# A ScalarE copy of the third product in three blocks of the last token half: what it does to the tail of an attention and maxout kernel

## The chip, the cores and the metric

The kernel runs on one core of one Trainium2 chip. The metric is the time of one execution on the device in microseconds (us). The runs of the kernel before lie within 1.2 us, so every statement below about hundredths of a us is about a stage inside one profiled execution, not about a total.

## The reference

```python
def _attn_ref(q, k, v, tau):                      # B, N, C = 4, 6144, 256
    qn = q / (norm(q, axis=1) + 1e-6); kn = k / (norm(k, axis=1) + 1e-6)
    a = softmax(kn.transpose(0, 2, 1) @ qn / tau)  # 256 x 256 for each batch
    return v @ a

def _moe_ref(x, w1, w2, w3, w_out):               # 24576 tokens, 256 -> 768 -> 256
    h = np.maximum(np.maximum(x @ w1, x @ w2), x @ w3)
    return h @ w_out
```

The function names `norm` and `softmax` stand for the written-out lines of the original. The second part, the maximum of three products and one more product, is nearly all of the work, and the change touches its last piece.

## The kernel before

The kernel folds the attention matrix into the three weights, so that each token needs three products with 256 x 768 weights, a maximum of the three, and a product with `w_out`. Tokens come in chunks of 512. For each 128-wide slice of the 768 columns, `h_block` makes three products in PSUM, the memory that takes TensorE's results, and takes their maximum with ScalarE and VectorE. In this cut and the next, three dots mark what is left out:

```python
    ps_h = ctx.enter_context(tc.tile_pool(name="ps_h", bufs=6, space=bass.MemoryType.PSUM))
    ...
    def h_block(gi, aw, fc, tsl=slice(0, TPC)):
        ...
        hp = []
        for m in range(3):
            t = htile(f"h_ps{m}")[:, :n]
            for ic in range(CC):
                PE.matmul(t..., lhsT=aw[m][:, ic, fsl], rhs=vt[:, tsl, ic, :],
                          start=(ic == 0), stop=(ic == CC - 1))
            hp.append(t)
        s_mx = mx_pool.tile([P, CHUNK], BF16, name="s_mx")[:, :n]
        ACT.activation(out=s_mx, in_=hp[0], func=AF.Copy)                  # L383
        DVE.tensor_tensor(out=s_mx, in0=hp[1], in1=s_mx, op=ALU.max)       # L384, first max
        DVE.tensor_tensor(out=ht, in0=hp[2], in1=s_mx, op=ALU.max)         # L385, second max
```

The products live in a pool of six PSUM banks. A product may be written only once the bank that it was given has been read by its last reader. The last chunk of 512 tokens is done in two halves of 256, so that the output of the first half can leave while the second is computed:

```python
        for fc in range(FC):                       # FC = 6 blocks of the first half
            h_block(gi, aw, fc, slice(0, HT))
            if 1 <= fc <= len(pending):
                pending[fc - 1]()                  # output products of the chunk before
        for fc in range(FC):                       # 6 blocks of the last half
            h_block(gi, aw, fc, slice(HT, TPC))
            if fc >= FC - HT:
                first_half(fc - (FC - HT))         # output products of the first half
        pss = [htile("o_ps") for _ in range(HT)]
        for fcs in (range(FC - 1), (FC - 1,)):
            for i in range(HT):
                products(pss[i], HT, i, fcs)       # output products of the last half
        ...                                        # two copies and two transfers out
```

"Block" below is one call of `h_block` in the last chunk; blocks 0 to 5 are the six of the last half.

Of the kernel before, what the change touches and what calls it, by code (L numbers as in the profile page):

```python
# [11 lines left out]
BF16 = mybir.dt.bfloat16  # L12
FP8 = mybir.dt.float8e4
AF = mybir.ActivationFunctionType
ALU = mybir.AluOpType
# [16 lines left out]
def kernel(  # L32
# [14 lines left out]
    DVE = nc.vector  # L47
    ACT = nc.scalar
# [6 lines left out]
    P = 128  # L55
    CC = C // P
    FC = d_ff // P
    CHUNK = 512
    TPC = CHUNK // P
# [20 lines left out]
    mx_pool = ctx.enter_context(tc.tile_pool(name="mx", bufs=4))  # L80
# [4 lines left out]
    def htile(name):  # L85
        return ps_h.tile([P, 512], FP32, tag="h", name=name)

    def xtile(name, cols=512, dtype=FP32):
        return ps_x.tile([P, cols], dtype, tag="x", name=name)
# [191 lines left out]
    def alloc_aw():  # L281
        return [aw_pool.tile([P, CC, d_ff], BF16, name=f"aw{m}_sb", tag=f"aw{m}") for m in range(3)]
# [83 lines left out]
        DVE.tensor_copy(out=vt[:, half:, :], in_=ps[:, half:, :])  # L366
        ACT.activation(out=vt[:, :half, :], in_=ps[:, :half, :], func=AF.Copy)

    def h_block(gi, aw, fc, tsl=slice(0, TPC)):

        vt = vts[gi]
        n = (tsl.stop - tsl.start) * P
        ht = hts[gi][:, fc, tsl.start * P:tsl.stop * P]
        fsl = slice(fc * P, (fc + 1) * P)
# [4 lines that stand above are left out]
                PE.matmul(t.rearrange("p (t n) -> p t n", n=P), lhsT=aw[m][:, ic, fsl], rhs=vt[:, tsl, ic, :],  # L379
                          start=(ic == 0), stop=(ic == CC - 1))  # L380
            hp.append(t)
        s_mx = mx_pool.tile([P, CHUNK], BF16, name="s_mx")[:, :n]
        ACT.activation(out=s_mx, in_=hp[0], func=AF.Copy)  # L383
        DVE.tensor_tensor(out=s_mx, in0=hp[1], in1=s_mx, op=ALU.max)  # L384
        DVE.tensor_tensor(out=ht, in0=hp[2], in1=s_mx, op=ALU.max)  # L385

    def o_steps(gi):

# [25 lines left out]
    def last_chunk(gi, aw, pending):  # L414

        hts[gi] = ht_pool.tile([P, FC, CHUNK], BF16, name="ht_sb")
        o_sb = o_pool.tile([P, TPC, d_model], FP32, name="o_sb")
        dst = out_r[gi // NCH, gi % NCH]
        HT = TPC // 2

        def products(ps, t0, i, fcs):
            c0 = i * d_model if t0 == 0 else 0
            for fc in fcs:
                PE.matmul(ps[:, c0:c0 + d_model], lhsT=hts[gi][:, fc, (t0 + i) * P:(t0 + i + 1) * P],  # L424
                          rhs=wo_sb[:, fc, :], start=(fc == 0 and c0 == 0), stop=(fc == FC - 1),
                          skip_group_check=True)

        first = {}

        def first_half(i):  # L430
            if i == 0:
                first["ps"] = xtile("o_ps")
            products(first["ps"], 0, i, range(FC))
            if i == HT - 1:
                ACT.activation(out=o_sb[:, 0:HT, :].rearrange("p t d -> p (t d)"), in_=first["ps"], func=AF.Copy)
                SP.dma_start(out=dst[:, 0:HT, :], in_=o_sb[:, 0:HT, :])

        for fc in range(FC):
            h_block(gi, aw, fc, slice(0, HT))
            if 1 <= fc <= len(pending):  # L440
                pending[fc - 1]()
        for fc in range(FC):
            h_block(gi, aw, fc, slice(HT, TPC))
            if fc >= FC - HT:
                first_half(fc - (FC - HT))
        pss = [htile("o_ps") for _ in range(HT)]
        for fcs in (range(FC - 1), (FC - 1,)):
            for i in range(HT):
                products(pss[i], HT, i, fcs)
        ACT.activation(out=o_sb[:, HT, :], in_=pss[0][:, 0:d_model], func=AF.Copy)  # L450
        DVE.tensor_copy(out=o_sb[:, HT + 1, :], in_=pss[1][:, 0:d_model])  # L451
        ACT.dma_start(out=dst[:, HT, :], in_=o_sb[:, HT, :])
        SP.dma_start(out=dst[:, HT + 1, :], in_=o_sb[:, HT + 1, :])
# [8 lines left out]
    aw = alloc_aw()  # L462
# [15 lines left out]
    for b in range(B):  # L478
# [3 lines left out]
        for ch in range(NCH):  # L482
            gi = b * NCH + ch
            if gi == B * NCH - 1:
                last_chunk(gi, aw, pending)
                break
# [23 lines left out]
            if more and 0 <= s0 < 8:  # L510
                g0 = s0 * 6
                for i, (which, g) in enumerate(((1, g0), (1, g0 + SQW), (0, g0), (0, g0 + SQW))):

                    last = not early and s0 == 7 and which == 0
# [17 lines left out]
            for fc in range(FC):  # L532
                h_block(gi, aw, fc)
                for f in gaps[fc]:
                    f()
# [12 lines left out]
            if more and ch == NCH - 1:  # L548
                et, rinv = st["e"], st["r"]
                aw = alloc_aw()  # L550
# [37 lines left out]
```

## Time and profile before

| | before |
|---|---|
| median of the first 3 runs | 573.58 us (573.29 to 574.51) |
| span of the profiled execution | 571.6 us |
| TensorE busy | 553.2 us, 97% |
| 36 products, 560.11 to 564.58 | 4.47 us (3.94 us if nothing waits) |
| from the first output product (564.58) to the end of TensorE's work (568.02) | 3.44 us |

A profile is read here in three steps. First, which engine is busy nearly all the time: TensorE. Second, where that engine is not: the chain of work that ended last names other engines only at the very start (GpSimd and the transfers of q) and in the last ten microseconds. Third, what ends those waits. The prediction below shows the lines. One more way of seeing a wait is worth learning. Matmuls are pipelined, and two undisturbed ones in a row cover 0.38 us in the timeline. Asked for in windows so narrow that only two show, the three waits of the kernel before are these lines (start, duration, count at the end):

```profile
561.85 0.38 PE L379 MATMUL h_ps<-vt_sb,aw_sb 128*128 128x256 bf16 x2
561.96 0.52 PE L379 MATMUL h_ps<-vt_sb,aw_sb 128*128 128x256 bf16 x2
562.76 0.59 PE L379 MATMUL h_ps<-vt_sb,aw_sb 128*128 128x256 bf16 x2
563.62 0.58 PE L379 MATMUL h_ps<-vt_sb,aw_sb 128*128 128x256 bf16 x2
```

The first line is an undisturbed pair. The others are longer by 0.14, 0.21 and 0.20 us, ahead of blocks 2, 3 and 4. That sums to 0.55 us, against 0.53 us by the count of matmuls in the prediction; the difference is rounding of the printed times.

What each wait is for can be read from the program after it is built: a product names the instruction whose end frees its bank. For block 2's first product, for example, that is the second max of the first half's last block, and for block 3's the second max of block 0. VectorE's second maxes of that stretch:

```profile
561.74 0.42 DVE L385 TENSOR_TENSOR ht_sb<-h_ps,s_mx 128x256 bf16<-128x256 f32 x1
562.60 0.42 DVE L385 TENSOR_TENSOR ht_sb<-h_ps,s_mx 128x256 bf16<-128x256 f32 x1
563.46 0.42 DVE L385 TENSOR_TENSOR ht_sb<-h_ps,s_mx 128x256 bf16<-128x256 f32 x1
```

TensorE goes on at 562.22 and 563.08, which is 0.06 us after the first of these maxes ends and 0.06 after the second.

ScalarE had idle time. In its timeline the value in brackets is its idle time before the instruction:

```profile
562.63 0.38 ACT L383 ACTIVATE s_mx<-h_ps 128x256 bf16<-128x256 f32 x1 [0.41 <-PE h_ps L379]
563.49 0.38 ACT L383 ACTIVATE s_mx<-h_ps 128x256 bf16<-128x256 f32 x1 [0.48 <-PE h_ps L379]
564.34 0.38 ACT L383 ACTIVATE s_mx<-h_ps 128x256 bf16<-128x256 f32 x1 [0.47 <-PE h_ps L379]
```

### The profile page before, as it was taken

The page shows a single profiled execution, that of the slowest core. Times are in us where ns is not written, and L with a number is a line of the kernel's source. Part 1 is how long each engine was busy: PE and PEld are TensorE (multiplying, and loading weights), DVE is VectorE, ACT ScalarE, POOL GpSimd, SP SyncE. Part 2 cuts the span into 40 slices and gives each one's busy share as a digit, 9 for nine tenths or more (in the row PEclk, how much of TensorE's full clock was granted, in tenths as well). Part 3 has the DMA queues.
Part 4 walks back from the last instruction along what each step waited for, and adds up shares of the span by engine and source line. Part 5 has one row for each costly group of instructions (what it writes and reads, how often), then busy time and mean ns, then how long its engine had stood idle before and what let it go on. Part 6 is the DMA issues. An engine that isn't in the chain of part 4 may idle for free.

```text
span 571.6 us, 9437 instructions
## 1 busy us (share of the span) xinstructions
PE 553.2 (97%) x3343; PEld 329.7 (58%) x3344; DVE 416.1 (73%) x658; ACT 309.5 (54%) x540; POOL 233.4 (41%) x237
## 2 busy tenths in 40 slices
PE   3789999999999999999999999999999999999997
PEld 2665555555755555555575555555575555555566
DVE  0048777877887778777767777777768778778775
ACT  1044567677464576776535467767645444444443
POOL 2441357776450078776560058776750000000000
PEclk9999999999999999999999999999999999999999
DMA  9995999884579168884279339984437233132112
GB/s 144 106 172 95 136 239 133 159 134 110 107 86 182 56 116 154 134 150 104 57 131 151 100 81 138 148 141 101 119 86 155 75 78 107 56 104 63 56 55 76
DMA packets 76960, 65.64 MB, mean 115 GB/s; under 512 B 52464, under 2 KB 62576, under 8 KB 76784
## 3 DMA queue, kind: packets, MB, share of 16 engines
q0 software_dynamic: 19072, 26.48, 38.6%
q1 hardware_dynamic: 57696, 38.41, 24.6%
q8 instruction: 26, 0.43, 0.3%
q14 instruction: 22, 0.18, 0.1%
q10 hardware_dynamic: 144, 0.13, 0.1%
HBM read 78.64 MB, written 25.17 MB: 182 GB/s over the span
## 4 chain that ended last, share of the span: by engine, by line
PE 93%; DMA 5%; POOL 0%; issue 0%; DVE 0%; POOLq 0%
PE h_ps L379 65%; PE o_ps L399 22%; DMA q_sb<-in_q_dram 5%; PE gram L250 3%; PE ew_ps L301 3%; POOL k_sb L99 0%; PE o_ps L424 0%; PE ew_ps L325 0%; PE warm_ps L459 0%; PE vt_ps L362 0%; PE gram L181 0%; DVE ht_sb L385 0%; DVE o_sb L451 0%; PE rs_ps L289 0%; PE gram L183 0%
## 5 line engine op out<-in xcount | busy, mean ns | idle before, releaser
L379 PE MATMUL h_ps<-vt_sb,aw_sb 128*128 128x512 bf16 (+1 forms) x1764 | 406.7, 375 | 0.1
L379 PEld LDWEIGHTS <-aw_sb 128*128 128x128 bf16 x1764 | 171.7, 98 | 161.7 <-DVE aw_sb L307 2.4
L384 DVE TENSOR_TENSOR s_mx<-h_ps,s_mx 128x512 bf16<-128x512 f32 (+1 forms) x294 | 198.9, 676 | 82.0 <-ACT s_mx L383 81.8
L383 ACT ACTIVATE s_mx<-h_ps 128x512 bf16<-128x512 f32 (+1 forms) x294 | 172.4, 586 | 124.1 <-PE h_ps L379 123.1
L385 DVE TENSOR_TENSOR ht_sb<-h_ps,s_mx 128x512 bf16<-128x512 f32 (+1 forms) x294 | 200.3, 681 | 30.6
L209 POOL TENSOR_TENSOR acc<-acc,sq 128x768 f32<-128x768 f32 x88 | 144.2, 1648 | 69.3 <-ACT sq L201 53.3
L399 PE MATMUL o_ps<-wo_sb,ht_sb 128*128 128x256 bf16 x1128 | 153.9, 273 | 0.0
L399 PEld LDWEIGHTS <-ht_sb 128*128 128x128 bf16 x1128 | 110.4, 98 | 52.1
L402 ACT ACTIVATE o_sb<-o_ps 128x512 f32<-128x512 f32 x94 | 56.1, 597 | 83.7 <-PE o_ps L399 83.7
L110 POOL DMA_DIRECT2D v_sb<-in_v_dram x48 | 27.8, 584 | 37.6 <-DMA vt_sb<-v_sb 35.4
L201 ACT ACTIVATE sq<-q_sb 128x768 bf16<-128x768 fp8e4 x48 | 40.5, 844 | 0.0
L201 ACT ACTIVATE sq<-k_sb 128x768 bf16<-128x768 fp8e4 x48 | 40.1, 835 | 0.0
L206 POOL CAST acc<-sq 128x768 f32<-128x768 bf16 x6 | 4.9, 820 | 65.0 <-ACT sq L201 65.0
L102 POOL DMA_DIRECT2D q_sb<-in_q_dram x33 | 18.4, 566 | 4.7 <-DMA v_sb<-in_v_dram 3.9
L169 PE MATMUL kk<-k_sb 128*128 128x256 fp8e4 x48 | 7.5, 338 | 11.8 <-DVE k_sb L155 6.4
L99 POOL DMA_DIRECT2D k_sb<-in_k_dram x29 | 16.1, 557 | 2.8 <-issue 1.1
L250 PE MATMUL gram<-k_sb,q_sb 128*128 128x512 fp8e4 x144 | 16.8, 276 | 0.0
L304 ACT ACTIVATE aw_sb<-ew_ps,rinv 128x384 bf16<-128x384 f32 (+1 forms) x24 | 13.2, 555 | 5.7 <-PE ew_ps L301 4.8
L250 PEld LDWEIGHTS <-q_sb 128*128 128x256 fp8e4 x144 | 15.9, 136 | 0.6
L222 POOL PARTITION_ALL_REDUCE tot<-acc x6 | 10.9, 1858 | 11.8 <-issue 5.9
L301 PE MATMUL ew_ps<-w_sb,et 128*128 128x384 bf16 (+1 forms) x96 | 15.6, 313 | 0.0
L181 PE MATMUL gram<-k_sb,q_sb 128*128 128x512 fp8e4 x48 | 11.4, 331 | 2.8 <-DMA q_sb<-in_q_dram 2.7
(64 smaller groups left out, 113.3 us busy)
## 6 DMA issues: line engine op xcount, KB each, us to landing
out_dram<-o_sb SPq DMA_DIRECT2D x41, 512.0 KB, 2.9
v_sb<-in_v_dram POOLq DMA_DIRECT2D x48, 256.0 KB, 4.1
k_sb<-in_k_dram POOLq DMA_DIRECT2D x24, 192.0 KB, 5.7
q_sb<-in_q_dram POOLq DMA_DIRECT2D x24, 192.0 KB, 7.1
out_dram<-o_sb SPq DMA_DIRECT2D x13, 256.0 KB, 2.0
k_sb<-in_k_dram POOLq DMA_DIRECT2D x5, 256.0 KB, 10.7
w_sb<-in_moe_w_dram POOLq DMA_DIRECT2D x9, 128.0 KB, 5.7
kf<-in_k_dram SPq DMA_DIRECT2D x1, 1024.0 KB, 4.9
```

The lines of the kernel that those rows point to most:

```text
L102: POOL.dma_start(out=qk[b][0][:, g0:g0 + w, :], in_=q_r[b][:, g0:g0 + w, :])
L110: POOL.dma_start(out=t, in_=v_r[gi // NCH, gi % NCH])
L201: ACT.activation(out=sq, in_=src, func=AF.Square)
L209: POOL.tensor_tensor(out=acc, in0=acc, in1=sq, op=ALU.add)
L250: PE.matmul(g[:, j * C:(j + 1) * C], lhsT=qt[:, tsl, j * P:(j + 1) * P], rhs=kt[:, tsl, :], start=(tp == 0 and j == 0), stop=(tp == NG // ...
L301: PE.matmul(ew[:, :w], lhsT=et[:, j, ic * P:(ic + 1) * P], rhs=w_sb[m][:, j, fsl], start=(j == 0), stop=(j == CC - 1))
L379: PE.matmul(t.rearrange("p (t n) -> p t n", n=P), lhsT=aw[m][:, ic, fsl], rhs=vt[:, tsl, ic, :], start=(ic == 0), stop=(ic == CC - 1))
L383: ACT.activation(out=s_mx, in_=hp[0], func=AF.Copy)
L384: DVE.tensor_tensor(out=s_mx, in0=hp[1], in1=s_mx, op=ALU.max)
L385: DVE.tensor_tensor(out=ht, in0=hp[2], in1=s_mx, op=ALU.max)
L399: PE.matmul(st["ps"][:, half], lhsT=ht[:, fc, t * P:(t + 1) * P], rhs=wo_sb[:, fc, :], start=(fc == 0), stop=(fc == FC - 1))
L402: ACT.activation(out=st["o"][:, t - 1:t + 1, :].rearrange("p t d -> p (t d)"), in_=st["ps"], func=AF.Copy)
```

## The change

The intent is to give VectorE less to do where TensorE waits for it. A second ScalarE copy puts the third product into SBUF as bf16, so the second max has both inputs there.

```diff
-    def h_block(gi, aw, fc, tsl=slice(0, TPC)):
+    def h_block(gi, aw, fc, tsl=slice(0, TPC), two_copies=False):
...
         DVE.tensor_tensor(out=s_mx, in0=hp[1], in1=s_mx, op=ALU.max)
-        DVE.tensor_tensor(out=ht, in0=hp[2], in1=s_mx, op=ALU.max)
+        last = hp[2]
+        if two_copies:
+            last = mx_pool.tile([P, CHUNK], BF16, name="s_h2")[:, :n]
+            ACT.activation(out=last, in_=hp[2], func=AF.Copy)
+        DVE.tensor_tensor(out=ht, in0=last, in1=s_mx, op=ALU.max)
...
         for fc in range(FC):
-            h_block(gi, aw, fc, slice(HT, TPC))
+            h_block(gi, aw, fc, slice(HT, TPC), two_copies=fc in (0, 2, 3))
```

The copy does two things at once. It makes the second max cheaper, and it frees the third product's PSUM bank without VectorE. Both kernels were built and their instructions compared engine by engine: apart from block 0's new copy, with the bank that it frees and the max that reads it, they are the same up to block 1 of the last half; from block 2 on the banks are handed out differently, and TensorE waits for other instructions.

## The prediction

> **What bounds the kernel now.** I read the page first, then the last microseconds: the change touches six blocks of the last chunk only (here a block is the three products of one 128-wide slice of d_ff for 256 tokens). From the page:
>
> ```profile
> PE 553.2 (97%) x3343; PEld 329.7 (58%) x3344; DVE 416.1 (73%) x658; ACT 309.5 (54%) x540; POOL 233.4 (41%) x237
> PEclk9999999999999999999999999999999999999999
> PE 93%; DMA 5%; POOL 0%; issue 0%; DVE 0%; POOLq 0%
> ```
>
> TensorE is busy 97% of the span at full clock, and 93% of the chain that ended last is TensorE; VectorE shows as 0%. So nearly all of the 573.58 us cannot be reached by a VectorE change. The question is what happens where this rule fails: in the tail. The chain that ended last, in order of time, for the last 17 us (start, duration, what):
>
> ```profile
> 559.61 0.66 PE o_ps L399 x6
> 560.27 2.34 PE h_ps L379 x20
> 562.61 0.43 DVE ht_sb L385
> 563.03 0.04 issue
> 563.08 0.82 PE h_ps L379 x6
> 563.89 0.03 issue
> 563.92 0.81 PE h_ps L379 x6
> 564.74 0.66 PE o_ps L424 x6
> 565.39 0.66 PE h_ps L379 x6
> 566.05 1.98 PE o_ps L424 x18
> 568.03 0.02 issue
> 568.05 0.42 DVE o_sb L451
> ```
>
> Here TensorE once waits for a second max (L385 at 562.61), and after that the blocks take 0.82 us in place of 0.66. The weight loads of the same stretch show all waits (in brackets: idle before):
>
> ```profile
> 562.22 0.64 PEld L379 LDWEIGHTS <-aw_sb 128*128 128x128 bf16 x6 [0.16 <-issue]
> 563.08 0.64 PEld L379 LDWEIGHTS <-aw_sb 128*128 128x128 bf16 x6 [0.22 <-issue]
> 563.93 0.53 PEld L379 LDWEIGHTS <-aw_sb 128*128 128x128 bf16 x5 [0.21 <-issue]
> ```
>
> Three waits, 0.59 us together. Counted by matmuls it is a little less: in the timeline 36 of them start from 560.11 and the next kind starts at 564.58; at the undisturbed pitch of 0.109 us (six in 0.656, as 564.58, 565.23 and 565.89 show) they would need 3.94, so 4.47 - 3.94 = 0.53 us is lost. I use 0.53. After 564.58 nothing is lost: the last 18 start at 565.89 and end at 568.02. So **0.53 us is the most that the change can win**, 0.09% of the time.
>
> The cause is VectorE's pace. Groups by form:
>
> ```profile
> L385 DVE TENSOR_TENSOR ht_sb<-h_ps,s_mx 128x512 bf16<-128x512 f32 x282 | 195.2, 692 | 29.4
> L385 DVE TENSOR_TENSOR ht_sb<-h_ps,s_mx 128x256 bf16<-128x256 f32 x12 | 5.1, 425 | 1.2
> L384 DVE TENSOR_TENSOR s_mx<-h_ps,s_mx 128x256 bf16<-128x256 f32 x12 | 5.0, 417 | 1.0 <-ACT s_mx L383 1.0
> L383 ACT ACTIVATE s_mx<-h_ps 128x256 bf16<-128x256 f32 x12 | 4.6, 383 | 4.8 <-PE h_ps L379 3.9 <-DVE ht_sb L385 0.9
> ```
>
> In the timeline VectorE's starts in the last half go 562.08 (first max), 562.60 (second), 562.94, 563.46 and so on: 0.525 us from first to second, which depends on it, and 0.335 on to the next block, which overlaps the end. That is 0.86 us a block against TensorE's 0.66. With six PSUM banks for products, TensorE runs two blocks ahead and then goes at VectorE's pace, until the two groups of output products (0.66 each, before and after the sixth block) give VectorE time to catch up.
>
> **What the Trainium skill says.** "VectorE: DVE Perf Modes", section "The perf-mode tier table": a two-tensor operation runs at 1x with any PSUM operand and at 2x with both in bf16 in SBUF. The kernel before has no bf16 pair in SBUF, so its trace cannot confirm the 2x. The same page's errata section gives an fp32 two-tensor operation (N+151)/0.96 ns: 424 ns for 256 and 691 for 512; the trace has 425 and 692, in agreement. Estimate of mine from page and trace for the packed form: 151 + 128 cycles at 0.96 GHz = 290 ns, a saving of 0.135 us an instruction. "ScalarE: Activation LUTs", section "What ACT_TABLE_LOAD costs": an activation with immediate scale takes 186 ns + 0.833 N, 399 for 256, and back-to-back ones overlap by about 93; the trace has 383. "SBUF — State Buffer", section "Who interferes with whom": a VectorE operation with two SBUF inputs contends with GpSimd reads. In the last 16 us GpSimd has 0.00 busy, so this should not arise.
>
> **The change part by part.** Added: three ScalarE copies of 0.38 us, in blocks 0, 2 and 3 of the last half (numbers from 0). Changed: three second maxes from 0.425 to about 0.29. VectorE's block then takes 0.86 - 0.135 = 0.725 us where changed. Moved: the third product's PSUM bank is freed by the ScalarE copy, not by the second max. And the listing of the built program shows that banks are handed out differently from block 2 on, so TensorE waits for other things. Everything before those blocks is instruction for instruction the same.
>
> I walk through the last half with the trace's delays: a product is readable 0.415 us after its first matmul starts (563.08 to ScalarE's 563.49), a freed bank lets TensorE go about 0.055 after the freeing ends, products are 0.219 apart.
> - Block 0 starts at 560.77, block 1 at 561.42, as before. ScalarE copies product 0 at 561.18, product 2 at 561.62 (0.77 + 0.44 + 0.415) until 562.00, and block 1's product 0 at about 561.93 until 562.31.
> - Block 2, product 0, took a bank freed by the first half's last second max (562.16, start 562.22). Now it takes the one freed by the new copy at 562.00: it starts at 562.08 without a wait. Product 1 waits for that max (562.22 < 562.30), product 2 for block 1's ScalarE copy (562.36 < 562.52). Wait 1, 0.15, is gone.
> - VectorE: block 0's second max runs 562.60 to 562.89, block 1's first max 562.81 to 563.22.
> - Block 3 starts at 562.73. Product 0 needs block 0's first max (562.49, fine), product 1 block 2's copy (562.88 + 0.055 against 562.95, just in time), product 2 block 1's first max: 563.28 against 563.17. **A wait of 0.11.**
> - VectorE: block 1's second max, not changed, 563.34 to 563.76.
> - Block 4: product 0 at 563.50 needs block 2's new copy (563.31, fine), product 1 block 1's second max: 563.82 against 563.72. **A wait of 0.10.** Product 2 at 564.03 needs nothing late.
> - Output products start at 564.25 in place of 564.58; block 5 at 564.91; the last 18 matmuls at 565.56.
> - VectorE goes on without a pause: the last second max ends near 566.94 (567.32 before). The last two matmuls need it at 567.31. So it does not set the end.
>
> Sum: 0.53 - 0.21 = 0.32 us won. After the last matmul the output copy and transfers (3.57 us of span) stay as they are and simply move earlier. 573.58 - 0.32 = **573.26 us**.
>
> **The rivals.**
> 1. The packed mode doesn't come, and the second max stays at 0.425. Then the new copy still frees banks: wait 1 goes, block 3 waits 0.24 for block 1's first max (563.41 against 563.17), block 4 0.09. Won: 0.53 - 0.33 = 0.20, giving 573.38. Against it: the aligned bf16 tiles are just what the page asks for.
> 2. ScalarE becomes the bound: two adjacent blocks, 2 and 3, carry two copies each, 2 x 0.38 - 0.09 = 0.67 us a block, just over TensorE's 0.66, and the copy of a third product stands ahead of the next block's first copy in its queue. Before, ScalarE idled 0.41 to 0.48 us ahead of each of these copies, so there is room for one more and nothing else. If each hand-over is 0.1 late at the new waits, the gain is used up: 573.5. If the last second max were late by more than the 0.37 us of slack in my walk, the time would be longer; I see nothing that large.
> 3. All waits vanish, as the bound allows: 573.05. For it: the waits left are only 0.1 each, the size of my errors. Against it: block 1 is not changed and still costs VectorE 0.86.
> 4. The end is set by a fixed transfer, and earlier products don't matter. Against it: the chain goes through the last matmul into the copy at 568.05, and the last transfer is issued at once after it.
>
> **Range and chances.** All of these lie between 573.05 and 573.6, and the spread of the three runs before (573.29 to 574.51) is larger than any of them. Hence 573.25, range 572.6 to 574.2, mostly for the spread. 2% is 11.5 us, twenty times the most that can be won, and the three copies of 1.15 us in all could not cost it even if wholly on the path: faster 0.005, same 0.99, slower 0.005.
>
> **What would show it.** Right, step by step: three second maxes near 0.29 us with SBUF inputs, nine still near 0.425; no idle time of the weight loads ahead of block 2, two short ones in blocks 3 and 4; 4.14 us in place of 4.47 from block 0's predecessor (560.11) to the first output product; the last 18 matmuls undisturbed; 3.5 us from the last matmul to the end as before. Wrong: a second max that starts late behind a ScalarE copy, waits of the weight loads adding up to 0.5 us or more, a wait inside the last 18 matmuls, or a change anywhere earlier in the span.

## The result, and the profile after

| | before | after |
|---|---|---|
| median of 4 runs | 573.54 us (573.29 to 574.51) | 573.12 us (572.86 to 573.55) |
| span of the profiled execution | 571.6 us | 571.7 us |
| 36 products before the first output product | 4.47 us | 4.14 us |
| first output product to the end of TensorE's work | 3.44 us | 3.44 us |
| end of TensorE's work to the end of the span | 3.60 us | 3.65 us |
| TensorE's waits in the tail | 0.14 + 0.21 + 0.20 us | 0.12 + 0.09 us |

The ratio of the times is 0.999, with a 95% interval of 0.9973 to 1.0008, which contains 1. By the totals alone the two kernels cannot be told apart. The stage can: in the profile it is shorter by 0.33 us.

The chain that ended last, of the changed kernel, from where the tail begins (start, duration, what):

```profile
560.67 4.14 PE h_ps L379 x36
564.81 0.66 PE o_ps L428 x6
565.47 0.66 PE h_ps L379 x6
566.12 1.98 PE o_ps L428 x18
568.10 0.02 issue
568.13 0.42 DVE o_sb L456
```

The second max and the two "issue" pieces of the kernel before are gone from it: 36 products now stand as one piece. That does not yet mean that nothing waits; the piece is 0.2 us longer than 36 x 0.109 = 3.94. The weight loads and the narrow windows of TensorE show where:

```profile
560.40 4.12 PEld L379 LDWEIGHTS <-aw_sb 128*128 128x128 bf16 x36
563.35 0.38 PE L379 MATMUL h_ps<-vt_sb,aw_sb 128*128 128x256 bf16 x2
563.46 0.50 PE L379 MATMUL h_ps<-vt_sb,aw_sb 128*128 128x256 bf16 x2
564.01 0.47 PE L379 MATMUL h_ps<-vt_sb,aw_sb 128*128 128x256 bf16 x2
```

The line of the weight loads, which before was cut into pieces by three waits, is now one piece, so this view alone would have said that no wait is left. The pairs of matmuls say otherwise: 0.12 us behind the fourth matmul of block 3 (the next, its third product, starts at 563.69) and 0.09 us behind the second of block 4.

The groups by form in the window of the tail, VectorE of the changed kernel (count, busy us, mean ns, idle before):

```profile
L389 DVE TENSOR_TENSOR ht_sb<-h_ps,s_mx 128x256 bf16<-128x256 f32 x4 | 1.7, 425 | 0.4
L389 DVE TENSOR_TENSOR ht_sb<-s_h,s_mx 128x256 bf16<-128x256 bf16 x3 | 0.9, 293 | 0.3
```

Three second maxes have bf16 inputs from SBUF only and take 293 ns; the others still take 425. ScalarE's new copies and VectorE's last instructions, in order of time:

```profile
562.02 0.39 ACT L388 ACTIVATE s_h<-h_ps 128x256 bf16<-128x256 f32 x1
562.30 0.38 ACT L383 ACTIVATE s_mx<-h_ps 128x256 bf16<-128x256 f32 x1
563.33 0.39 ACT L388 ACTIVATE s_h<-h_ps 128x256 bf16<-128x256 f32 x1
564.10 0.39 ACT L388 ACTIVATE s_h<-h_ps 128x256 bf16<-128x256 f32 x1
```

```profile
563.22 0.42 DVE L384 TENSOR_TENSOR s_mx<-h_ps,s_mx 128x256 bf16<-128x256 f32 x1
563.74 0.42 DVE L389 TENSOR_TENSOR ht_sb<-h_ps,s_mx 128x256 bf16<-128x256 f32 x1
566.92 0.42 DVE L389 TENSOR_TENSOR ht_sb<-h_ps,s_mx 128x256 bf16<-128x256 f32 x1
568.13 0.42 DVE L456 COPY o_sb<-o_ps 128x256 f32<-128x256 f32 x1 [0.78 <-PE o_ps L428]
```

**Why the span did not get shorter.** The profiled execution of the changed kernel has a span 0.1 us longer than that of the kernel before, though its tail is 0.33 us shorter. Its tail began 0.4 us later (560.51 against 560.11), and the instructions up to there are the same; its end, after TensorE's last matmul, took another 0.05 us more (3.65 against 3.60). The chain of the kernel before, at its start (start, duration, what), and then that of the changed kernel:

```profile
20.81 12.94 DMA q_sb<-in_q_dram
33.80 0.32 PE gram L181
```

```profile
21.39 12.57 DMA q_sb<-in_q_dram
34.00 0.32 PE gram L181
```

The first load of q released TensorE 0.2 us later. Another 0.2 us comes from one wait of the weight loads between 60 and 155 us; the line below is what the waits of the changed kernel show there, and the kernel before shows none. It ends at 79.7 us; up to there TensorE is 0.2 us later than in the kernel before, from there on 0.4 us:

```profile
PEld L379 <- DMA vt_sb<-v_sb: 0.5, 1, 0.5
```

So in this pair of profiles a difference of transfers in the first 100 us is as large as what the tail won. The other three runs of the changed kernel have spans of 571.1, 571.4 and 571.3 us.

### The profile page after: what moved, and what is told of

Its sections match the earlier page's. It is cut to its first block, busy times and chain, and to the rows that moved or that the text cites. A ratio compares the mean times of both kernels' runs of the same rounds, so it can differ in the third digit from the quotient of the medians. Undisturbed runs are those within 1.5% of the kernel's fastest.

```text
span 571.7 us, 9440 instructions
## 1 busy us (share of the span) xinstructions
PE 553.0 (97%) x3343; PEld 329.8 (58%) x3344; DVE 415.7 (73%) x658; ACT 310.4 (54%) x543; POOL 233.6 (41%) x237
## 4 chain that ended last, share of the span: by engine, by line
PE 93%; DMA 5%; POOL 0%; issue 0%; DVE 0%; POOLq 0%
PE h_ps L379 65%; PE o_ps L403 22%; DMA q_sb<-in_q_dram 5%; PE gram L250 3%; PE ew_ps L301 3%; POOL k_sb L99 0%; PE o_ps L428 0%; PE ew_ps L325 0%; PE warm_ps L464 0%; PE vt_ps L362 0%; PE gram L181 0%; DVE o_sb L456 0%; PE rs_ps L289 0%; PE gram L183 0%; PE rs_ps L319 0%
## 5 line engine op out<-in xcount | busy, mean ns | idle before, releaser
L250 PE MATMUL gram<-k_sb,q_sb 128*128 128x512 fp8e4 x144 | 16.8, 277 | 0.0
L169 PEld LDWEIGHTS <-k_sb 128*128 128x256 fp8e4 x48 | 6.4, 182 | 13.3 <-DMA k_sb<-in_k_dram 7.1
```

The lines of the kernel that those rows point to most:

```text
L250: PE.matmul(g[:, j * C:(j + 1) * C], lhsT=qt[:, tsl, j * P:(j + 1) * P], rhs=kt[:, tsl, :], start=(tp == 0 and j == 0), stop=(tp == NG // ...
```

## The experiments

None of the experiments ran on a chip, and what they were to tell apart is therefore open where the two traces do not settle it. The first four kernels were refused before they ran: they contain the double-row matmul mode of the fp8 products of q and k, as the kernel before and the changed kernel do, and that mode was held back on the day. They were rebuilt with two plain matmuls for each double-row one, far ahead of the tail, and built without faults, but in sixteen attempts spread over almost five hours (block 3 alone four times, the kernel before in the same form four, the fp32 copy three, blocks 0, 1 and 2 five) no chip ran one; whether that was for want of a chip or because the kernel before, which runs beside each experiment, has the same mode, could not be found out. The plan is told here with the numbers on record, because a reader can take it up.

**Block 3 alone.** The edit against the changed kernel:

```diff
-two_copies=fc in (0, 2, 3)
+two_copies=fc == 3
```

Expected: 

> Only block 3 has the second copy. Theory: block 3's bank and block 3's max are not what TensorE waits for in any of its three waits, so the stage takes 4.47 us as before with waits near 0.14, 0.21 and 0.20 us, although that max takes 0.29 us. Rival (each copied block gives a third of the gain): 4.36 us.

Measured: nothing. What the traces say in its place is under the last point of the next section.

**The copy without the packed max.** The copy goes to fp32. It is meant to leave the second max at 0.42 us, so that the copy only frees the bank; no run shows that it would.

```diff
-            last = mx_pool.tile([P, CHUNK], BF16, name="s_h2")[:, :n]
+            last = mx_pool.tile([P, CHUNK], FP32, name="s_h2")[:, :n]
```

Expected: 

> The three copies go to fp32 in SBUF[...]. Theory (the freed bank and the shorter max both count): these three second maxes take 0.42 us, the wait ahead of block 2 is gone, one wait of about 0.25 us is left in block 3, the stage takes 4.19 us, and the last two matmuls wait about 0.06 us for the last second max. Rival (only VectorE's speed counts): 4.47 us as before. Rival (only the bank counts): 4.14 us as in the changed kernel.

Measured: nothing. It would have separated the two things that the copy does.

**Blocks 0, 1 and 2.**

```diff
-two_copies=fc in (0, 2, 3)
+two_copies=fc in (0, 1, 2)
```

Expected: 

> Blocks 0, 1 and 2 have the second copy in place of 0, 2 and 3. Theory: the two waits left are for block 1's first and second max, which come 0.13 us sooner or are replaced by its copy once block 1 has the copy too, so no wait is left: the stage takes 3.94 us, 0.2 us less than the changed kernel, and the median is about 0.5 us under the kernel before. Rival (ScalarE, with two copies in three adjacent blocks and 0.67 us a block, becomes the bound): waits of 0.05 us or more stay, stage above 4.05 us.

Measured: nothing. It is the version that the two traces point to as better than both kernels; that it is better is an inference, not a measurement.

**The changed kernel again, five rounds.** Expected: 

> The changed kernel once more, for its time. The 36 products from the first half's sixth block to the first output product took 4.47 us before and 4.14 us in the changed kernel's first profile. My theory (the tail's waits of TensorE are all that changed): 4.14 us again, waits of 0.12 and 0.11 us in blocks 3 and 4, and 0.3 us less than before in the median, with single runs scattering by 0.3 us or more from the start of the kernel. Rival (the 0.4 us between the medians is scatter): the stage repeats, but the medians of this call differ by less than 0.1 us or the other way.

Measured: nothing. Whether the 0.42 us between the medians is the 0.33 us of the tail or scatter stays open; the interval holds both.

## Why the prediction was right or wrong

The total, 573.12 us against 573.25 predicted, is right, but this proves little: any of the rivals fits into the scatter too. What tests the reasoning is the tail, step by step. The tail of the changed kernel starts 0.40 us later than that of the kernel before, so 0.40 is added to each predicted start and end below (not to durations).

| step of the prediction | predicted | measured |
|---|---|---|
| packed second max | 0.29 us | 0.293 us |
| wait ahead of block 2 | gone | gone |
| waits ahead of blocks 3 and 4 | gone | gone |
| wait in block 3, ahead of its third product | 0.11 us | 0.12 us |
| wait in block 4, ahead of its second product | 0.10 us | 0.09 us |
| 36 products | 4.14 us | 4.14 us |
| block 0's new copy starts | 562.02 | 562.02 |
| block 1's first max starts | 563.21 | 563.22 |
| block 1's second max starts | 563.74 | 563.74 |
| end of the last second max | 567.34 | 567.34 |
| waits in the last 18 matmuls | none | none |
| from the last matmul to the end | 3.5 us, as before | 3.65 us (before: 3.60) |

**One reading that does not hold.** The steps of the forecast held. Its account of the kernel before does not hold throughout: it puts all three waits there down to VectorE's pace. For the third the program waits for ScalarE: block 4's first product has the bank of block 3's first product, whose copy starts 0.41 us after block 3's first matmul (563.08 to 563.49) and ends 0.79 us after it, while block 3's products take 0.66 us. With that hand-out of banks a shorter max alone would have left this wait at nearly 0.2 us, by an estimate from these times. The forecast did not suffer, because its walk took the banks of the changed kernel from the built program.

**Where each wait went.** Block 2's first product now gets the bank freed by block 0's new copy, which ends at 562.41. Block 2's first matmul is the 19th of the 36 and, if nothing waits, due at 560.51 + 18 x 0.109 = 562.47; so the bank is ready in time, if by little, and the narrow windows show no long pair there. Block 3's first product now gets a bank freed by block 0's first max (562.49 + 0.41 = 562.90, used at 563.13), and block 4's one freed by block 2's new copy (563.33 + 0.39 = 563.72, used at 563.90). So all three old waits are gone. The two that are left were hidden behind them: the products of the same place waited for the same two instructions in the kernel before, but reached them late enough. The one of 0.12 us ends at 563.69, and block 1's first max ends at 563.22 + 0.42 = 563.64. The one of 0.09 us ends at 564.22, and block 1's second max, the one that was not made cheaper, ends at 563.74 + 0.42 = 564.16. In both cases TensorE goes on 0.05 to 0.06 us after the end, as it did before. These are the banks that the built program makes those products wait for. What is left is thus put down to block 1 by the program's waits and by the times of the trace, not by an experiment.

**What is not separated.** The changed kernel differs in three things at once: banks are freed earlier, they are handed out in another order, and three maxes are shorter. How much of the 0.33 us each one wins, no run shows. The prediction's walk for its first rival gives 0.20 us for the banks without the shorter max, an estimate.

**The rivals.** That the packed mode would not come is refuted: 293 ns. The trace agrees with the page "VectorE: DVE Perf Modes", section "The perf-mode tier table", on that, and the estimate of 290 ns, with the fixed term of the same page's errata section, was close. That ScalarE would become the bound is refuted for this choice of blocks, though it had been what one wait of the kernel before was for: its idle time has shrunk, but its copies run up to 0.03 us earlier than in the walk (562.30 against 562.33), and neither of the two waits left is for a ScalarE copy. That all waits vanish is refuted, with 0.21 us left. That the end is set by a fixed transfer is not refuted by totals, which scatter too much; in the trace the last copy starts 0.04 us after the last matmul's end (568.09 to 568.13), against 0.03 before (568.02 to 568.05). Contention of the packed max with GpSimd could not be seen, for GpSimd is busy for 0.00 us in the tail; so this case says nothing about it.

**What block 3's copy is worth.** The prediction counted three copies and did not ask what each wins. In the changed kernel TensorE does not wait at all after 564.22, while block 3's copy runs from 564.10 and its max only from 565.33. In a build with the copy in blocks 0 and 2 alone, the products of block 5 get banks that are freed by block 2's first max, block 4's first copy and block 3's first max; by the times of the changed kernel's trace the latest of these is block 3's first max, with its end at 564.81 + 0.42 = 565.23, ahead of block 5's start at 565.30. VectorE's last max ends at 567.34; without the saving in block 3 it would end 0.13 us later, near 567.47, and the last two matmuls, due at 565.96 + 16 x 0.109 = 567.70, would still find it done. So the third copy of the change seems to be worth nothing. This is argued from the trace and a build; a run of blocks 0 and 2 alone did not happen.

## What to carry to other kernels

Where one engine is busy for 97% of the time, look for the few stretches in which it is not, and take from them the upper bound of what a change can win before asking how; here 0.53 us of 573. All five waits followed here ended with the release of a buffer. So find, in the built program, which instruction frees the buffer that the waiting engine gets next, before deciding which engine to relieve: one of the three waits before was for ScalarE, although VectorE had the slower pace. Expect the hand-out of buffers to change with the program, and waits that were hidden behind the removed ones to appear. When the expected gain is below the scatter of the runs, compare a stage between two fixed events in the traces, and say that the total settles nothing.

## What the Trainium skill lacked or had wrong

- "VectorE: DVE Perf Modes", the errata section, gives 58 + N/2 cycles (N/Accel, with 2 for this mode) for a packed operation from SBUF and then corrects the fixed term to about 150 in its text; for a 256-element bf16 max the run shows 293 ns, which fits (128 + 151)/0.96 = 290 ns and not (58 + 128)/0.96 = 194 ns. The table's figure is thus not the duration that the profile shows; from the start of such a max to the start of the next, independent one it is 0.21 us (563.01 to 563.22).
- The same page, section "The DRAIN you can't avoid", finds, for eight copies, that semaphores between VectorE operations cost nothing extra; it does not say what it costs to read the result of the operation before. In the kernel before a max that depends on the one before starts 0.11 us after its end (562.08 + 0.41 to 562.60), an independent one 0.08 us before it (562.60 + 0.42 to 562.94), so the dependent one comes 0.19 us later. No run separates the semaphore from the wait for the data.
- No page gives the time from the end of the reader of a PSUM bank to the first matmul into that bank: it was 0.05 to 0.06 us in all five waits followed here.
- "ScalarE: Activation LUTs", section "What ACT_TABLE_LOAD costs", gives 186 ns + 0.833 N, which is 399 ns for such a copy of 256; the traces show means of 381 to 385 ns.
